# A second buffer for the converted w_a and w_b tiles of the first block

## The chip, the cores and the metric

The kernel runs on one core of one Trainium2 chip. The metric is the device time of one execution in microseconds. A number for a change is the median of several timed runs; the profile comes from one more execution, recorded by the hardware profiler, and has a time of its own.

## The reference

Three parts follow each other. Attention with a local window: 4 batches of 8 heads, 512 local and 32 global positions, head size 64; its output is a matrix x of 2304 tokens by 512. Then two feed-forward blocks:

```python
h = x @ w_in                                   # 512 -> 2048
g = where(h >= 1, h, where(h <= -1, 0, (h + 1) ** 2 / 4))
x = g @ w_out                                  # 2048 -> 512
# second block
a, b = x @ w_a, x @ w_b                        # 512 -> 1536, twice
out = (a * b) @ w_out                          # 1536 -> 512
```

The weights come in as float64, read as pairs of 32-bit words. The change concerns w_a and w_b, of 512 x 1536 each, and only their way from float64 in HBM to float32 in HBM.

## The kernel before

Tokens are cut into six tiles, five of 384 and one of 256 (a local block of 128 and the 128 global rows). The first block runs over 96 units (t, f): tile t and one of 16 slices f of the hidden size. `h_unit` makes the hidden slice with 12 matmuls of 128 x 384 into `hp` (L410 to L412) and applies the activation on ScalarE and Vector (L682 to L688); `x_unit`, two units behind, adds the slice's part of the output with 12 more matmuls into `acc`. Every matmul is threefold, since operands are split into a high and a low part.

Attention for the next tile is put between these units, one item (a block and a pair of heads) at a time: scores (L173), row minimum on Vector (L186), exponential on ScalarE (L190), normalisation (L194 to L197), transposes (L203), their copy on ScalarE (L207), the output matmuls (L213) and their copy to `xraw` (L217). From block 6 on an item also splits q and k (L160, L161).

Weights of the first block (w_in, w_out) are loaded, converted and split during tile 0, out of a pool with three raw and three converted buffers. The pool is closed when tile 1 begins, and a new one, `pc`, serves w_a and w_b: two buffers for `wraw`, the loaded tile of 128 x 512 float64, and one for `wt`, the converted tile of 128 x 512. They are turned into float32 and written to HBM (`wd`), 24 tiles in all, so that the second block can load them at half the size and several times over. The code asks for one of them in every other unit of tiles 1, 2 and 3:

```python
if i + 1 < len(ab2):
    w_load(*ab2[i + 1])                        # the load ahead, L89
(nm, f2), tf = w_conv()
nc.sync.dma_start(wd[f2]["ab".index(nm)], tf)  # L735
```

`w_conv` (L92) takes a `wt` buffer and does four instructions: L97 on ScalarE scales the high word's float, L98 shifts the bits on Vector, L99 puts the sign in, L100 the low word's bits. L97 needs the loaded tile and a free `wt` buffer. A raw buffer is free again after L100, a `wt` buffer after the write has landed. The second block reads `wd` through L500.

All these loads and writes, and those of q and k (L153) and v (L165), go through SyncE's queue. The order in which instructions stand on each engine is not that of the code: Tile puts it together when the program is built, out of the code's order, the data that each instruction needs, the buffers that are free and estimated durations. After that each engine keeps its order, and a waiting instruction holds up those behind it.

The other pools: PSUM has four buffers each for tags `h` and `acc`; `qk` has three buffers and `v` four.

Of the kernel before, what the change touches and what calls it, by code (L numbers as in the profile page):

```python
# [58 lines left out]
def body(tc, qk, vw, kg, vg, w1i, w1o, w2a, w2b, w2o, mask, out):  # L59
# [24 lines left out]
    sp = {}  # L84
    wslots = {}

    def w_load(key, src):
        raw = sp["p"].tile([P, 512, 2], I32, name="wraw", bufs=sp["raw"])
        nc.sync.dma_start(raw, src.bitcast(I32).rearrange("p (f two) -> p f two", two=2))  # L89
        wq.append((key, raw))  # L90

    def w_conv():  # L92
        key, raw = wq.pop(0)
        low, high = raw[:, :, 0], raw[:, :, 1]
        t = sp["p"].tile([P, 512], I32, name="wt", bufs=sp["wt"])
        tf = f32(t)
        nc.scalar.activation(tf, f32(high), AF.Copy, scale=W_DOWN)  # L97
        nc.vector.tensor_scalar(t, t, 3, 0x7FFFFFFF, ALU.logical_shift_left, ALU.bitwise_and)  # L98
        nc.vector.scalar_tensor_tensor(t, high, -0x80000000, t, ALU.bitwise_and, ALU.bitwise_or)  # L99
        nc.vector.scalar_tensor_tensor(t, low, 29, t, ALU.logical_shift_right, ALU.bitwise_or)  # L100
        return key, tf
# [282 lines left out]
    def x_split(t, W):  # L384
        hi, lo = [], []
        last = t == len(TILES) - 1
        for c in range(NC):
            pool = x5p if last else mp
            h = pool.tile([P, W if last else 384], F32R, name=f"xh{c}", bufs=1)
            l = pool.tile([P, W if last else 384], F32R, name=f"xl{c}", bufs=1)  # L390
            src = xraw_cur[t][c]
            nc.scalar.activation(h[:, :W], src[:, :W], AF.Copy)
            nc.vector.tensor_tensor(l[:, :W], src[:, :W], f32(h[:, :W]), ALU.subtract)  # L393
            hi.append(h)
            lo.append(l)
        return hi, lo

    def widths(t):
        return P * len(TILES[t])
# [50 lines left out]
    def x1_load(s):  # L450
        n = half_cols(s)
        t0, t1 = PAIRS[s]
        w0 = widths(t0)
        for h in range(2):
            for c in range(NC):
                r = mp.tile([P, 384], F32, name=f"x1r{h}{c}", tag=f"xh{c}" if h else f"xraw{c}", bufs=1)
                lo, hi = h * n, (h + 1) * n
                if lo < w0:
                    e = min(hi, w0)
                    nc.sync.dma_start(r[:, :e - lo], x1d[t0][c, :, lo:e])  # L460
                if hi > w0:
                    b0 = max(lo, w0)
                    nc.sync.dma_start(r[:, b0 - lo:n], x1d[t1][c, :, b0 - w0:hi - w0])
                xr[(h, c)] = r
# [28 lines left out]
    wt = {}  # L493

    def ab_load(u):

        s, f = divmod(u, NF2)
        for i in range(2):
            t = sp["p"].tile([P, 512], I32, name="wt", bufs=sp["wt"])
            nc.sync.dma_start(f32(t), wd[f][i])  # L500
            wt[(u, i)] = f32(t)
# [38 lines left out]
    def raw_to(n):  # L540
        while rawi[0] < min(n, len(ws2)):
            w_load(*ws2[rawi[0]])
            rawi[0] += 1
# [123 lines left out]
    def h_unit(t, f):  # L667
        W = widths(t)
        if t not in xs:
            xs[t] = x_split(t, W)  # L670
        hi, lo = xs[t]
        w = wslots[("i", f)]
        hp = ps.tile([P, 512], F32, name="hp", tag="h")
        for c in range(NC):
            s = slice(c * P, (c + 1) * P)
            mm3(hp[:, :W], w[:, 0, s], w[:, 1, s], hi[c][:, :W], lo[c][:, :W], c == 0, c == NC - 1)
        flush()
        r = mp.tile([P, 384], F32, name="r", tag="r", bufs=3)
        m = mp.tile([P, 384], F32, name="m", bufs=2)
        g = mp.tile([P, 2, 384], F32R, name="g", tag="g", bufs=3)  # L680
        gh, gl = g[:, 0], g[:, 1]
        nc.scalar.activation(r[:, :W], hp[:, :W], AF.Relu, bias=half, scale=0.5 / W_UP)  # L682
        nc.vector.scalar_tensor_tensor(m[:, :W], hp[:, :W], 1.0 / W_UP, r[:, :W], ALU.mult, ALU.max)  # L683
        nc.vector.scalar_tensor_tensor(m[:, :W], r[:, :W], 1.0, m[:, :W], ALU.min, ALU.mult)  # L684

        def fin():
            nc.scalar.activation(gh[:, :W], m[:, :W], AF.Copy)  # L687
            nc.vector.tensor_tensor(gl[:, :W], m[:, :W], f32(gh[:, :W]), ALU.subtract)  # L688
        deferred.append(fin)
        gq[(t, f)] = (gh, gl)  # L690
# [23 lines left out]
    for u in range(len(units)):  # L714
        for kind in (0, 1):
            if kind == 0:
                if u >= len(units):
                    continue
                t, f = units[u]
                if t == 0:  # L720
                    while W1.si < min(2 * f + LEAD1, len(ws1)):
                        W1.step()
                if t == 1 and f == 0:
                    es_st.close()
                    gp["k"] = es_att.enter_context(tc.tile_pool(name="kp", bufs=1, reuse_waits="tile"))
                    sp["p"] = es_st.enter_context(tc.tile_pool(name="pc", bufs=1, reuse_waits="tile"))
                    sp["raw"], sp["wt"] = 2, 1
                if 1 <= t <= 3 and f % 2 == 0:
                    i = 8 * (t - 1) + f // 2
                    if i == 0:  # L730
                        w_load(*ab2[0])
                    if i + 1 < len(ab2):
                        w_load(*ab2[i + 1])
                    (nm, f2), tf = w_conv()
                    nc.sync.dma_start(wd[f2]["ab".index(nm)], tf)  # L735
                if t == len(TILES) - 2 and f == 0:
                    es_st.close()
                    gp["p"] = es_att.enter_context(tc.tile_pool(name="gp", bufs=1, reuse_waits="tile"))
                if f == 0 and t + 1 < nt:
                    n_items = ends[t + 1] - done["n"]  # L740
                    rate = 3.0 * n_items / (2 * (GLOB_END if t == nt - 2 else NF1) - 1)
                    credit = 0.0
                if (t, f) == (nt - 2, GLOB_END):
                    for _ in att:
                        pass
                    es_att.close()
                    sp["p"] = es_st.enter_context(tc.tile_pool(name="st2", bufs=1, reuse_waits="tile"))
                    sp["raw"], sp["wt"] = RAWBUFS, 4
                    x5p = es_st.enter_context(tc.tile_pool(name="x5p", bufs=1, reuse_waits="tile"))
                    raw_to(RAWBUFS)  # L750
                    ab_load(0)
                if t == nt - 1 and f == 0:
                    xs[t] = xs_last
                h_unit(t, f)
                if (t, f) == (nt - 2, GLOB_END + 1):
                    xs_last = x_split(nt - 1, widths(nt - 1))
                if t == nt - 1:
                    if f == 0:
                        x1_load(0)
                    elif f == 1:  # L760
                        ab_sum(0)
                        ab_load(1)
                    elif f in (2, 3):
                        ab_split(0, 2 * f - 4)
                        ab_split(0, 2 * f - 3)
                    elif f == 4:
                        x_pre(0)
                    if f >= 5 and f < 12:
                        x_op(0, f - 5)
                    elif f == 14:  # L770
                        ab_sum(1)
                        ab_split(1, 0)
                    elif f == 15:
                        for part in range(1, 4):
                            ab_split(1, part)
            else:
                if u < LAG:
                    continue
                tx, fx = units[u - LAG]
                x_unit(tx, fx)  # L780
            if u < len(units) and t + 1 < nt:
                credit += rate
                while credit >= 1.0 and done["n"] < ends[t + 1]:
                    credit -= 1.0
                    att_step(ends[t + 1])
        if u < len(units) and f == NF1 - 1 and t + 1 < nt:
            while att_step(ends[t + 1]):
                pass
# [95 lines left out]
```

## Time and profile before

| | us |
|---|---|
| median of 3 runs | 979.52 |
| lowest and highest | 978.26, 979.92 |
| profiled execution, time | 985.52 |
| profiled execution, span | 983.7 |

| engine | busy us | share of the span |
|---|---|---|
| TensorE, matmuls (PE) | 943.9 | 96% |
| TensorE, weight loads (PEld) | 842.4 | 86% |
| Vector (DVE) | 709.4 | 72% |
| ScalarE (ACT) | 527.4 | 54% |

Busy time is the time in which at least one instruction of the engine runs; matmuls overlap in the pipeline. The span goes from the first to the last instruction, and the execution's own time has 1.8 us more. In the rows, PE is TensorE's matmuls, PEld its weight loads, DVE Vector, ACT ScalarE, SP SyncE; a q behind the name is the engine's queue. L12 is line 12 of the kernel, and "a <- b" behind an operation is what it writes and reads.

### The profile page before, as it was taken

How to read it: one execution, taken by the hardware profiler on the slowest of the kernel's cores; microseconds unless marked ns; L12 is line 12 of the kernel's file. 1: busy time of each engine (PE TensorE's matmuls, PEld its weight loads, DVE VectorE, ACT ScalarE, POOL GpSimd, SP SyncE). 2: the span in 40 equal slices, each digit the busy share in tenths (PEclk: the TensorE clock that was granted, in tenths of full speed). 3: DMA queues.
4: the chain of work that ended last, by engine and by line, in shares of the span. 5: the costliest groups of instructions: out<-in, count | busy, mean ns of one | idle time of the engine just before them, and what ended most of it. 6: DMA issues, size and time to landing. Idle time of an engine off the chain costs nothing.

```text
span 983.7 us, 16767 instructions
## 1 busy us (share of the span) xinstructions
PE 943.9 (96%) x6044; PEld 842.4 (86%) x6044; DVE 709.4 (72%) x1841; ACT 527.4 (54%) x1253; POOL 0.7 (0%) x7
## 2 busy tenths in 40 slices
PE   7899888998999999999999999999999999999997
PEld 4587677886988898898879999999999999999996
DVE  6699998877875565565446878888796666887673
ACT  7667676555555555454444655555554444644441
POOL 0000000000000000000000000000000000000000
PEclk9699999999999999999999999999999999999999
DMA  7456546554551111103435323331241111042101
GB/s 232 133 168 200 170 164 198 189 181 161 189 169 37 44 62 49 29 16 105 146 112 200 113 71 118 109 95 43 58 147 54 43 44 54 22 140 54 55 12 54
DMA packets 55843, 104.28 MB, mean 106 GB/s; under 512 B 6864, under 2 KB 28496, under 8 KB 55760
## 3 DMA queue, kind: packets, MB, share of 16 engines
q1 hardware_dynamic: 55616, 103.05, 33.6%
q8 instruction: 47, 0.77, 0.3%
q14 instruction: 36, 0.29, 0.1%
q10 hardware_dynamic: 144, 0.17, 0.1%
HBM read 87.99 MB, written 15.20 MB: 105 GB/s over the span
## 4 chain that ended last, share of the span: by engine, by line
PE 75%; DVE 10%; DMA 9%; ACT 4%; issue 2%; ACTq 0%; SPq 0%; DVEq 0%
PE hp L410 5%; PE pb L567 5%; PE pb L568 5%; PE py L632 5%; PE pb L565 5%; PE py L633 5%; PE hp L412 5%; PE acc L410 5%; PE py L631 5%; PE hp L411 5%; DMA wd<-wt 5%; PE acc L411 4%; PE acc L412 4%; PE px L565 4%; PE px L568 4%; PE px L567 4%
## 5 line engine op out<-in xcount | busy, mean ns | idle before, releaser
L410 PE MATMUL hp<-xh,w 128*128 128x384 f32 (+1 forms) x384 | 133.8, 348 | 9.7 <-DVE m L683 3.8
L410 PE MATMUL acc<-g,w 128*128 128x384 f32 (+1 forms) x384 | 133.7, 348 | 3.0 <-ACT g L687 3.0
L411 PE MATMUL acc<-g,w 128*128 128x384 f32 (+1 forms) x384 | 127.7, 333 | 0.0
L412 PE MATMUL hp<-xl,w 128*128 128x384 f32 (+1 forms) x384 | 127.2, 331 | 0.0
L411 PE MATMUL hp<-xh,w 128*128 128x384 f32 (+1 forms) x384 | 126.4, 329 | 0.0
L412 PE MATMUL acc<-g,w 128*128 128x384 f32 (+1 forms) x384 | 125.5, 331 | 0.0
L107 ACT ACTIVATE w<-wt 128x512 fp32r<-128x512 f32 (+1 forms) x116 | 65.0, 564 | 72.2 <-PE pb L568 44.8
L567 PE MATMUL pb<-w 128*128 128x384 f32 (+1 forms) x288 | 94.6, 329 | 0.0
L568 PE MATMUL pb<-w 128*128 128x384 f32 (+1 forms) x288 | 94.3, 327 | 0.0
L565 PE MATMUL pb<-w 128*128 128x384 f32 (+1 forms) x288 | 93.8, 326 | 0.0
L410 PEld LDWEIGHTS hp<-xh,w 128*128 128x128 f32 x384 | 73.0, 190 | 19.9 <-DVE m L683 5.8
L683 DVE SCALAR_TENSOR_TENSOR m<-hp,r 128x384 f32<-128x384 f32 (+1 forms) x96 | 50.9, 530 | 51.4 <-ACT r L682 51.4
L682 ACT ACTIVATE r<-hp,half 128x384 f32<-128x384 f32 (+1 forms) x96 | 53.4, 557 | 62.6 <-PE hp L412 61.9
L410 PEld LDWEIGHTS acc<-g,w 128*128 128x128 f32 x384 | 73.1, 190 | 11.7 <-issue 5.4
L687 ACT ACTIVATE g<-m 128x384 fp32r<-128x384 f32 (+1 forms) x96 | 48.3, 503 | 63.3 <-DVE m L684 63.0
L632 PE MATMUL py<-w,g 128*128 128x512 f32 x204 | 80.7, 396 | 0.0
L633 PE MATMUL py<-w,g 128*128 128x512 f32 x204 | 80.7, 396 | 0.0
L631 PE MATMUL py<-w,g 128*128 128x512 f32 x204 | 79.6, 390 | 0.0
L108 DVE TENSOR_TENSOR w<-wsum,w 128x256 fp32r<-128x256 f32 (+1 forms) x108 | 54.6, 507 | 29.3 <-ACT w L107 29.3
L411 PEld LDWEIGHTS acc<-g,w 128*128 128x128 f32 x384 | 73.1, 190 | 1.6 <-issue 1.0
L412 PEld LDWEIGHTS acc<-g,w 128*128 128x128 f32 x384 | 72.8, 190 | 1.3 <-issue 1.1
L412 PEld LDWEIGHTS hp<-xl,w 128*128 128x128 f32 x384 | 73.1, 190 | 0.8 <-DVE xl L393 0.5
(112 smaller groups left out, 2093.2 us busy)
## 6 DMA issues: line engine op xcount, KB each, us to landing
wt<-wd SPq DMA_DIRECT2D x72, 256.0 KB, 2.6
qk<-in_qk_dram SPq DMA_DIRECT2D x64, 176.0 KB, 2.5
wraw<-in_w1i_dram SPq DMA_DIRECT2D x16, 512.0 KB, 3.6
wraw<-in_w1o_dram SPq DMA_DIRECT2D x16, 512.0 KB, 4.0
v<-in_vw_dram SPq DMA_DIRECT2D x64, 112.0 KB, 2.6
wraw<-in_w2a_dram SPq DMA_DIRECT2D x12, 512.0 KB, 4.6
wraw<-in_w2b_dram SPq DMA_DIRECT2D x12, 512.0 KB, 3.8
wd<-wt SPq DMA_DIRECT2D x24, 256.0 KB, 2.2
```

Of the source, the lines that this page charges most:

```text
L107: nc.scalar.activation(hi, src, AF.Copy)
L108: nc.vector.tensor_tensor(lo, src, f32(hi), ALU.subtract)
L410: nc.tensor.matmul(acc, whi, xhi, start=first, stop=False)
L411: nc.tensor.matmul(acc, wlo, xhi, start=False, stop=False)
L412: nc.tensor.matmul(acc, whi, xlo, start=False, stop=last)
L565: nc.tensor.matmul(out[:, :n], w[:, 0, r], hi[:, c, :n], start=start and c == 0, stop=False, skip_group_check=True)
L567: nc.tensor.matmul(out[:, :n], w[:, 1, r], hi[:, c, :n], start=False, stop=False, skip_group_check=True)
L568: nc.tensor.matmul(out[:, :n], w[:, 0, r], lo[:, c, :n], start=False, stop=k in (1, 5, 6) and c == 1, skip_group_check=True)
L631: nc.tensor.matmul(a, gh[:, c], w[:, 0], start=f == 0, stop=False)
L632: nc.tensor.matmul(a, gh[:, c], w[:, 1], start=False, stop=False)
L633: nc.tensor.matmul(a, gl[:, c], w[:, 0], start=False, stop=f == NF2 - 1)
L682: nc.scalar.activation(r[:, :W], hp[:, :W], AF.Relu, bias=half, scale=0.5 / W_UP)
```

## The change

The `wt` tag of the pool `pc` gets a second buffer, from tile 1 to the end of the 24 conversions. The pool grows by 2 KB per partition. The code of a conversion and the number of raw buffers stay.

```diff
@@ -724,7 +724,7 @@
                     es_st.close()
                     gp["k"] = es_att.enter_context(tc.tile_pool(name="kp", bufs=1, reuse_waits="tile"))
                     sp["p"] = es_st.enter_context(tc.tile_pool(name="pc", bufs=1, reuse_waits="tile"))
-                    sp["raw"], sp["wt"] = 2, 1
+                    sp["raw"], sp["wt"] = 2, 2
                 if 1 <= t <= 3 and f % 2 == 0:
                     i = 8 * (t - 1) + f // 2
                     if i == 0:
```

## Rows read from the trace of the kernel before

**Rows 1.** Busy us per engine (x instructions) by stage; clock, DMA share, GB/s

```profile
core 0: us, PE busy (x) PEld busy (x) DVE busy (x) ACT busy (x) POOL busy (x), PEclk, DMA share, GB/s
100.00:140.00 40.00, 33.28 (x200) 27.88 (x200) 37.60 (x94) 26.18 (x56) 0.00 (x0) 1.00 0.57 170
160.00:170.00 10.00, 8.03 (x56) 6.92 (x56) 8.18 (x25) 6.48 (x16) 0.00 (x0) 1.00 0.73 244
150.49:287.47 136.98, 124.37 (x799) 109.90 (x798) 108.66 (x309) 81.06 (x203) 0.00 (x0) 0.98 0.57 181
287.47:446.18 158.71, 158.71 (x1058) 142.23 (x1058) 92.92 (x285) 84.18 (x214) 0.00 (x0) 1.00 0.17 49
```

**Rows 2.** The same view, ten microseconds of it

```profile
200.00:210.00 10.00, 9.49 (x55) 8.73 (x56) 8.22 (x22) 5.50 (x13) 0.00 (x0) 0.83 0.49 176
```

**Rows 3.** Shares of the chain of waits from 150 to 290 us

```profile
by line: DMA wd<-wt 31.8%; DVE wt L99 10.5%; DVE wt L100 9.0%; ACT wt L97 8.4%; issue 7.0%; DVE wt L98 5.4%; DVE m L683 4.4%; ACT e L190 3.0%; DVE g L688 2.5%; DVE e L186 2.3%; DVE qkl L161 2.0%; DVE m L684 1.8%; ACT r L682 1.6%; DVE sm L19
```

**Rows 4.** SyncE in order of time: start us, us

```profile
175.64 0.33 SPq L735 DMA_DIRECT2D wd<-wt  x1
176.08 0.36 SPq L89 DMA_DIRECT2D wraw<-in_w2a_dram  x1
...
181.46 0.34 SPq L735 DMA_DIRECT2D wd<-wt  x1
```

**Rows 5.** ScalarE in order of time, with the idle before and what ended it

```profile
177.85 0.67 ACT L97 ACTIVATE wt<-wraw 128x512 f32<-128x512 f32 x1 [0.85 <-DMA wd<-wt]
```

**Rows 6.** Who waited for whom, 140 to 290 us: total us, times, longest

```profile
ACT wt L97 <- DMA wd<-wt: 19.8, 15, 3.7
...
PE tp L203 <- DVE xraw L217: 4.1, 3, 1.7
...
PE s L173 <- ACT pt L207: 2.0, 2, 1.4
PE o L213 <- DVE mn L186: 2.0, 2, 1.1
...
PE o L213 <- DVE m L683: 1.7, 2, 0.9
...
ACT qkh L160 <- DMA qk<-in_qk_dram: 0.2, 1, 0.2
```

**Rows 7.** Instructions on wd: duration ns, first and last start us

```profile
L500 SPq DMA_DIRECT2D wt<-wd x72: 319/320/654, 519.9 to 935.4; - x72
L735 SPq DMA_DIRECT2D wd<-wt x24: 319/327/458, 150.5 to 287.0; - x24
```

**Rows 8.** A group on TensorE, 150.49 to 287.47 us: busy us, mean ns

```profile
L410 PE MATMUL acc<-g,w 128*128 128x384 f32 x80 | 29.4, 368 | 0.0
```

**Rows 9.** Vector in order of time

```profile
173.40 0.42 DVE L98 TENSOR_SCALAR wt<-wt 128x512 int32<-128x512 int32 x1
173.85 0.69 DVE L99 SCALAR_TENSOR_TENSOR wt<-wraw,wt 128x512 int32<-128x512 int32 x1
174.46 0.55 DVE L688 TENSOR_TENSOR g<-m,g 128x384 fp32r<-128x384 f32 x1
174.93 0.69 DVE L100 SCALAR_TENSOR_TENSOR wt<-wraw,wt 128x512 int32<-128x512 int32 x1
175.53 0.38 DVE L186 CUSTOM_DVE_ANT_0 e<-s,masks 128x224 f32<-128x224 f32 x1
```

**Rows 10.** DMA issues from 150.49 to 287.47 us: KB each, median us to landing

```profile
wraw<-in_w2a_dram SPq DMA_DIRECT2D x11, 512.0 KB, 4.6
wraw<-in_w2b_dram SPq DMA_DIRECT2D x11, 512.0 KB, 3.7
```

**Rows 11.** What SyncE's DMA issues waited for, whole execution

```profile
SPq L735 <- DVE wt L100: 33.2, 8, 6.7
```

**Rows 12.** Who waited for whom, whole execution

```profile
ACT wt L97 <- DMA wraw<-in_w1o_dram: 6.8, 6, 3.1
...
ACT wt L97 <- DMA wraw<-in_w1i_dram: 3.0, 3, 2.0
```

## Prediction

> **What bounds the kernel now.** I read the busy times by stage first. From 287.47 to 446.18 us TensorE has no idle time and Vector is busy 92.92 of 158.71 us, 58.5% [rows 1]. In the 136.98 us ahead of it, from the first to behind the last write of a converted tile to HBM, TensorE is busy 124.37 us and Vector 108.66, 79% [rows 1]. So this stretch holds 136.98 - 124.37 = 12.6 us of TensorE idle. The ten-microsecond stretches show two lapses of its clock, a granted 0.83 from 200 to 210 us, in the row shown, and the same from 270 to 280: about a third of each at 1.2 GHz and the rest at 2.4, 10 x 0.17 = 1.7 us of work lost each time, 3.4 together, some of which may fall into the idle [rows 2]. The reader should see a ceiling: the loss that this stretch can give back is at most 12.6 + 3.4 = 16.0 us.
>
> Then the chain of waits from 150 to 290 us. The write of a converted tile (L735) is 31.8% of it, and the four conversion instructions L97 to L100 are 8.4 + 5.4 + 10.5 + 9.0 = 33.3% [rows 3]. Two thirds of the chain is one loop: convert, write, wait for the landing, convert the next. The loop can be followed in single rows: SyncE issues the write at 175.64, ScalarE's next L97 starts at 177.85 after 0.85 us of idle that the write ended, and the next write goes out at 181.46 [rows 4, 5]. Over the stretch ScalarE waited for such a landing 15 times, 19.8 us [rows 6]. There are 24 writes between 150.5 and 287.0 us, 136.5 / 23 = 5.93 us apart, and nothing reads them before 519.9 [rows 7].
>
> The code asks for one conversion every other unit over the 48 units of tiles 1 to 3. The stretch with all 24 holds 80 of the first matmuls of an accumulation into acc, four to a unit, so 20 units [rows 8]. Tile's ordering therefore draws conversions forward to where their data and buffers allow it, and the engines' fixed order then has every one of these waits in front of softmax and activation work.
>
> **The change part by part.** It adds one tile of 512 float32 per partition and removes, for conversion i, the wait for write i-1; write i-2 is waited for instead. No instruction is added: 24 conversions and 24 writes of 256 KB stay. The second buffer's first use comes after the conversions of the first tile are over, so it costs nothing; were it to wait there, one wait of the kind of rows 6 is the bound, 19.8 / 15 = 1.3 us, which I leave out.
>
> What the wait costs cannot be more than the 16.0 us above, nor less than nothing. ScalarE's 19.8 us are no price: TensorE works through part of them.
>
> Where does the stall go? Two things are late next. One is Vector. From start to start a conversion holds it 0.45 us (L98, 173.40 to 173.85), 0.61 (L99, to 174.46) and 0.60 (L100, 174.93 to 175.53), 1.66 together [rows 9]. Where TensorE is full, the other work leaves 41.5% of Vector, so a conversion fits every 1.66 / 0.415 = 4.0 us. The other is the loop through the two raw buffers. SyncE issues the next raw load right behind the write, 0.44 us after it [rows 4]; it lands after 4.6 or 3.7 us, median of the two kinds, 4.15 as their mean [rows 10]; ScalarE takes 0.67 [rows 5], Vector 1.66 with nothing between and, by the example above, 181.46 - 177.85 = 3.6 from ScalarE's start to the write. Two conversions then take 0.44 + 4.15 + 0.67 + 1.66 = 6.9 to 0.44 + 4.15 + 3.6 = 8.2 us, 3.5 to 4.1 each. Both give 4.0 us. I take 24 x 4.0 = 96 us for the conversions in place of 137.
>
> How much does TensorE lose in these 96 us? Bounds: nothing (the stretch without conversions loses nothing), and 20% (the worst ten microseconds, 160 to 170, where TensorE was busy 8.03) [rows 1]. Between them I take today's rate, 16.0 / 136.98 = 11.7%, because Vector will be fuller (about 98% instead of 79%) while the loop through the write is gone, and I cannot see either outweigh the other. Loss after: 96 x 0.117 = 11.2 us. Gain: 16.0 - 11.2 = 4.8 us. Behind the stretch TensorE is full, so the gain passes to the end. The profiled execution took 985.52 us (983.7 of span and 1.8 around it), so 980.7 by its clock; it ran 6.0 us over the median of the three timed runs, 979.52, and I take the gain from that: **974.7 us**.
>
> TensorE's busy time overlaps between matmuls, so the size of the loss can also be read from its weight loads: 109.90 / 136.98 = 80.2% in the stretch against 142.23 / 158.71 = 89.6% behind it [rows 1]. The Trainium skill (Perfetto Trace Analysis, Identifying the Most-Contended Engine) says that matmul busy time misjudges the distance from the roofline and that the weight loads' share is to be used. By it the loss is 136.98 - 109.90 / 0.896 = 14.4 us, the gain 14.4 x 0.30 = 4.3, and the time 975.2; this trace can't tell the two sums apart.
>
> On SyncE the writes and raw loads move ahead of loads of qk and v. A write waits at the head of that queue for its L100, 33.2 us in eight such waits [rows 11], with those loads behind it. ScalarE waited only 0.2 us for a qk [rows 6], so they are covered by the three and four buffers of these tiles; if that cover went, each late qk would cost some of one landing.
>
> **The rivals.**
> *All of it comes back.* The chain of waits speaks for it: two thirds are the loop that is cut. The raw loads may wait little: in tile 0, with three raw buffers, ScalarE waited 6.8 + 3.0 = 9.8 us for 32 raw loads, 0.31 each [rows 12]; 24 such are 7.4 us against 19.8. Were TensorE's loss to shrink alike, 16.0 x 7.4 / 19.8 = 6.0 stays and 10.0 comes back, 969.5; with nothing left, 963.5. Against it: two raw buffers, not three, and a fuller Vector.
>
> *Nothing comes back.* TensorE's own idle is not put down to the write: 4.1 us to the copy of an attention output (L217), 2.0 to ScalarE's L207, 2.0 to L186 and 1.7 to L683, 9.8 of 12.6 [rows 6]. These are delays of attention steps on two busy engines, and they could stay for the same total, or the raw loop could take the write loop's place. Time 979.5. The Trainium skill (Perfetto Trace Analysis, Identifying Performance Opportunities) says that improving a kernel generally means improving its most-contended engine; TensorE is that here and the edit doesn't touch it, which would be this case.
>
> *Vector becomes the bound, and it is slower.* Conversions drawn forward at one per 4.0 us fill Vector to 98%, and each may hold up an attention or activation step by up to 0.6 us, on which TensorE's PSUM banks wait. From 100 to 140 us, where Vector is busy 37.60 of 40, TensorE is busy 33.28, 83% [rows 1]; some of that is for weights needed at once. At the 20% of the worst stretch: 96 x 0.20 = 19.2, and 3.4 x 96 / 137 = 2.4 for the clock, 21.6 in all, 5.6 more than now: 985.1. It decides from a loss of (16.0 + 2.0) / 96 = 19% on; from 17% on the gain is gone.
>
> **How the numbers follow.** A change of 0.2% (2.0 us) is about what a measurement of this kernel can tell. Forecast (gain of 2 to 9 us): 0.45, with its own range 970.5 to 977.5. All comes back (9 to 16): 0.17. Nothing (within 2): 0.16. Slower: 0.22. So faster 0.62, same 0.16, slower 0.22. For 8 in 10 the range goes from 965, most of the first rival, to 984, over half of the slower one.
>
> **What would show each step.** In the trace after: ScalarE's L97 waiting for the write near nothing instead of 19.8 us, and some 5 to 12 us for raw loads; the 24 writes over about 96 us, the last near 245 us; Vector above 90% there and near 60% from there on; TensorE idle some 9 us in it and none behind it; the write gone from the chain. The prediction is wrong upward if TensorE's idle in the stretch is over 15 us, above all behind Vector; it is wrong downward if the order spreads the conversions and TensorE idles under 5 us. It is wrong in kind if the write stays in the chain, or if the new order moves time in the parts behind 290 us, where I assume nothing.

## The result, and the profile after

| | us |
|---|---|
| before, median of 5 runs | 979.44 |
| after, median of 5 runs | 984.90 (982.89 to 986.57) |
| after / before | 1.0052, 95% interval 1.0035 to 1.0069 |
| profiled execution after, time and span | 984.9, 983.1 |

The change makes the kernel slower by 0.5%. The two profiled executions take nearly the same, 985.52 and 984.9, but the one before reached its first write of a converted tile 5.2 us later (150.49 against 145.32 us), ahead of anything that the change touches. From that write to the end of the span it is 833.2 us before and 837.8 after.

Busy times by stage answer to [rows 1]: the stretch from the first to behind the last write, and what follows it up to the end of tile 3. Columns: TensorE, its weight loads, Vector, ScalarE, GpSimd, then granted clock, DMA share, GB/s.

```profile
145.32:247.97 102.65, 85.23 (x536) 74.31 (x535) 84.41 (x235) 58.45 (x146) 0.00 (x0) 0.95 0.68 220
247.97:446.18 198.21, 198.21 (x1316) 178.04 (x1316) 117.40 (x357) 106.44 (x268) 0.00 (x0) 1.00 0.17 50
```

The 24 conversions take 102.65 us in place of 136.98. In them TensorE idles 102.65 - 85.23 = 17.4 us, against 12.6, and the granted clock is 0.95: 0.05 x 102.65 = 5.1 us lost, against 3.4 by the two lapses in the prediction (by the mean clock of that stretch, 0.02 x 136.98 = 2.7). So the loss is up to 22.5 us in place of 16.0. Behind the stretch TensorE is full, as before. Vector is busy 84.41 of 102.65, 82%: it is not full. The two ten-microsecond stretches in which TensorE is busy least, and the one with the lowest clock, which answer to [rows 2]:

```profile
160.00:170.00 10.00, 6.71 (x40) 5.72 (x39) 6.59 (x20) 4.78 (x12) 0.00 (x0) 0.85 0.72 225
...
200.00:210.00 10.00, 6.61 (x43) 5.61 (x43) 7.60 (x23) 5.22 (x14) 0.00 (x0) 1.00 0.65 202
210.00:220.00 10.00, 8.73 (x49) 7.79 (x50) 7.64 (x21) 5.75 (x15) 0.00 (x0) 0.83 0.68 227
```

The write is still issued 24 times, and nothing waits for it any more; the last one goes out at 247.5 us, 4.44 us apart, in place of 287.0 and 5.93 [rows 7]:

```profile
L735 SPq DMA_DIRECT2D wd<-wt x24: 326/327/551, 145.3 to 247.5; - x24
```

What took its place is to be seen in the chain of waits from 140 to 255 us, which answers to [rows 3]:

```profile
by line: DMA wraw<-in_w2a_dram 40.2%; DVE wt L100 8.2%; DVE wt L99 7.4%; ACT wt L97 5.9%; issue 5.1%; DVE e L186 4.4%; DVE wt L98 3.8%; DVE qkl L161 2.6%; PE hp L410 2.2%; DVE m L683 2.1%; PE hp L411 1.7%; PE hp L412 1.7%; DVE xl L393 1.6%;
```

The write is gone from it and the load of a w_a tile, absent before, is 40.2%. Who waited for whom, 140 to 260 us, answers to [rows 6]:

```profile
ACT wt L97 <- DMA wraw<-in_w2a_dram: 20.0, 10, 3.3
DVE wt L98 <- ACT wt L97: 14.0, 16, 2.5
...
PE o L213 <- DVE mn L186: 5.5, 4, 3.3
...
PE s L173 <- DVE m L683: 3.7, 4, 1.5
...
ACT wt L97 <- DMA wraw<-in_w2b_dram: 0.8, 2, 0.5
```

ScalarE waited 20.8 us for raw loads, where it had waited 19.8 for writes. The wait moved one buffer back, at full size. It doesn't stay on ScalarE: L98 of the conversion stands in Vector's own order, and Vector waited there for the late L97 in 16 places, 14.0 us of its 102.65 - 84.41 = 18.2 us of idle. The kernel before has the same line, 140 to 290 us:

```profile
DVE wt L98 <- ACT wt L97: 16.1, 16, 2.1
```

One such wait can be followed to TensorE, in rows of ScalarE, Vector and TensorE:

```profile
205.68 0.67 ACT L97 ACTIVATE wt<-wraw 128x512 f32<-128x512 f32 x1 [3.27 <-DMA wraw<-in_w2a_dram]
...
206.37 0.43 DVE L98 TENSOR_SCALAR wt<-wt 128x512 int32<-128x512 int32 x1 [1.97 <-ACT wt L97]
...
207.44 0.38 DVE L186 CUSTOM_DVE_ANT_0 e<-s,masks 128x224 f32<-128x224 f32 x1
...
207.89 0.66 PE L213 MATMUL o<-pt,v 112*64 112x128 f32 x8 [1.18 <-DVE mn L186]
```

L97 is late by a load, Vector stands before L98, an attention item's L186 behind it is late, and TensorE waits for that. How a late L97 comes about shows in single rows, SyncE first, then ScalarE (compare [rows 4, 5]):

```profile
209.21 0.33 SPq L735 DMA_DIRECT2D wd<-wt  x1
209.63 0.38 SPq L89 DMA_DIRECT2D wraw<-in_w2a_dram  x1
...
213.52 0.33 SPq L735 DMA_DIRECT2D wd<-wt  x1
```

```profile
210.43 0.66 ACT L97 ACTIVATE wt<-wraw 128x512 f32<-128x512 f32 x1
210.99 0.52 ACT L687 ACTIVATE g<-m 128x384 fp32r<-128x384 f32 x1
214.56 0.67 ACT L97 ACTIVATE wt<-wraw 128x512 f32<-128x512 f32 x1 [3.06 <-DMA wraw<-in_w2a_dram]
```

At 209.63 SyncE issues a w_a load, right behind the write of the conversion that freed its raw buffer. The w_b tile in the other buffer is converted at 210.43. The instruction after the next is already L97 for the load just issued, and it stands at the head of the queue from 211.5 to 214.56, 3.06 us, with the softmax of an attention item behind it. The order put this L97 where a load would have to land in about 2 us (209.63 to 211.5); it took 4.9. Why the order did so is not shown; that it reckoned with shorter loads is a guess from this place. The loads themselves are as long as before [rows 10]:

```profile
wraw<-in_w2a_dram SPq DMA_DIRECT2D x11, 512.0 KB, 4.6
wraw<-in_w2b_dram SPq DMA_DIRECT2D x11, 512.0 KB, 3.6
```

### The profile page after: what moved, and what is told of

The parts are those of the page before. It is cut to its first block, busy times and chain, and to the rows that moved or that the text cites. A ratio compares the mean times of both kernels' runs of the same rounds, so it can differ in the third digit from the quotient of the medians.

```text
span 983.1 us, 16759 instructions
## 1 busy us (share of the span) xinstructions
PE 941.9 (96%) x6044; PEld 842.3 (86%) x6044; DVE 710.5 (72%) x1841; ACT 527.3 (54%) x1253; POOL 0.7 (0%) x7
## 4 chain that ended last, share of the span: by engine, by line
PE 80%; DVE 8%; DMA 7%; ACT 3%; issue 1%; SPq 0%; ACTq 0%; DVEq 0%
PE hp L410 6%; PE acc L410 5%; PE hp L412 5%; PE hp L411 5%; PE acc L411 5%; PE pb L567 5%; PE pb L568 5%; PE pb L565 5%; PE py L632 5%; PE py L633 5%; PE acc L412 5%; DMA wraw<-in_w2a_dram 5%; PE py L631 5%; PE px L565 4%; PE px L568 4%; PE px L567 4%
## 5 line engine op out<-in xcount | busy, mean ns | idle before, releaser
L410 PEld LDWEIGHTS hp<-xh,w 128*128 128x128 f32 x384 | 73.5, 191 | 18.2 <-DVE m L683 4.4
L410 PEld LDWEIGHTS acc<-g,w 128*128 128x128 f32 x384 | 72.7, 189 | 11.9 <-issue 5.8
L411 PEld LDWEIGHTS acc<-g,w 128*128 128x128 f32 x384 | 72.8, 190 | 1.6 <-issue 1.0
L411 PEld LDWEIGHTS hp<-xh,w 128*128 128x128 f32 x384 | 73.9, 192 | 0.0
```

The source lines that it names most:

```text
L410: nc.tensor.matmul(acc, whi, xhi, start=first, stop=False)
L411: nc.tensor.matmul(acc, wlo, xhi, start=False, stop=False)
```

## The experiments

Two theories stood against each other: that the loss comes from L97 waiting at the head of ScalarE's queue for something not yet landed (A), and that it comes from conversions crowding Vector and ScalarE (B). Times are medians; ratios are to runs of the kernel before on the same chip. Conversions are held back by a hold on the order: L97 of conversion i may be queued on ScalarE only behind the activation of a given unit.

```diff
-        nc.scalar.activation(r[:, :W], hp[:, :W], AF.Relu, ...)
+        relus.append(nc.scalar.activation(r[:, :W], hp[:, :W], AF.Relu, ...).ins)
...
-                    (nm, f2), tf = w_conv()
+                    with tc.issue_after(relus[NF1 + i - 1]):       # one per unit
+                        (nm, f2), tf = w_conv()
```

In the table, "apart" is the distance of the writes, first to last over 23; "L97 waits" is what ScalarE waited there for loads and writes; "idle" is TensorE's idle from 140 to 430 us of the profiled execution, a window that holds the writes of every kernel. In three kernels (raw3_wt1, half_raw4_wt3, half_raw4_unit08) the view puts some waits of L97 down to Vector or to "issue"; in each of these the write that frees the buffer landed 0.1 us or less before L97 began, so they are counted as waits for the write. In the kernels with half loads, L97 is L104 and L98 is L105 in the rows.

| kernel | raw, wt | apart us | L97 waits us | idle us | time us | ratio to before, 95% |
|---|---|---|---|---|---|---|
| before | 2, 1 | 5.93 | 19.8 | 12.6 | 979.44 | |
| after | 2, 2 | 4.44 | 20.8 | 17.4 | 984.90 | 1.0052 (1.0035 to 1.0069) |
| raw3_wt1 | 3, 1 | 5.93 | 19.9 | 13.2 | 978.44 | 0.9981 (0.9965 to 0.9997) |
| unit1_wt1, one per unit | 2, 1 | 6.20 | 15.9 | 8.7 | 976.58 | 0.9958 (0.9940 to 0.9975) |
| unit1_wt2, one per unit | 2, 2 | 5.74 | 0.5 | 1.9 | 964.67 | 0.9854 (0.9827 to 0.9882) |
| unit2_wt1, one per two units | 2, 1 | 11.3 | 0 | 1.6 | 964.97 | 0.9839 (0.9817 to 0.9861) |
| unit2_wt2, one per two units | 2, 2 | 11.3 | 0 | 1.5 | 964.52 | 0.9844 (0.9808 to 0.9881) |
| unit08_wt2, five per four units | 2, 2 | 5.23 | 11.1 | 11.0 | 979.46 | 0.9994 (0.9976 to 1.0011) |
| half_raw2_wt2, half loads | 2, 2 | 4.08 | 16.8 | 14.4 | 982.41 | 1.0021 (1.0001 to 1.0040) |
| half_raw4_wt2, half loads | 4, 2 | 3.38 | 8.2 | 8.8 | 972.82 | 0.9931 (0.9909 to 0.9953) |
| half_raw4_wt3, half loads | 4, 3 | 3.11 | 12.0 | 9.5 | 977.46 | 0.9966 (0.9947 to 0.9985) |
| raw3_y2 | 3, 2 | in bursts | 15.9 | 10.2 | 974.51 | 0.9936 (0.9915 to 0.9958) |
| half_raw4_unit08, five per four units | 4, 2 | 4.83 | 4.3 | 5.6 | 972.83 | 0.9923 (0.9893 to 0.9953) |
| half_raw4_unit1, one per unit | 4, 2 | 5.77 | 0 | 2.4 | 965.16 | 0.9857 (0.9830 to 0.9884) |
| half_raw4_unit08_no_l99 | 4, 2 | 4.57 | 0.3 | 1.5 | 964.67 | 0.9834 (0.9811 to 0.9858) |
| after_no_l99 | 2, 2 | 3.78 | 14.9 | 12.5 | 980.61 | 1.0002 (0.9983 to 1.0020) |

### The raw buffer alone

```diff
-                    sp["raw"], sp["wt"] = 2, 2
+                    sp["raw"], sp["wt"] = 3, 1
```

> Three raw buffers and one converted buffer: the raw buffer alone, without the change. Theory A (waits in the fixed order: the loss comes from L97 standing at the head of ScalarE's queue before the thing it waits for has landed): the write loop still binds as in the kernel before, L97 waits 15 to 25 us for the write, time 977 to 982. Theory B (crowding: the loss comes from how many conversions per microsecond Vector and ScalarE get, waits or not): conversions stay one per 5.9 us, time 979.5 as before.

Writes still 5.93 us apart, and a gain of 0.2% whose interval ends just short of nothing. The waits, 140 to 290 us:

```profile
ACT wt L97 <- DMA wd<-wt: 14.7, 13, 3.7
...
ACT wt L97 <- issue: 3.7, 1, 3.7
...
ACT wt L97 <- DVE x L709: 1.5, 1, 1.5
```

With the two that the view names otherwise, 14.7 + 3.7 + 1.5 = 19.9 us of waits for writes, as many as before, and as A expected. The write loop did bind the kernel before, as read from its chain.

### One conversion per unit, with one buffer and with two

The hold above, with `2, 1` and `2, 2`.

> One converted buffer, and conversion i is queued on ScalarE behind the activation of unit 16 + i - 1, so at most one per unit, about the pace that the kernel before has in the trace (one per 5.9 us). Theory A: the write loop (5.7 us) is just as long as a unit with its attention item (5.65), so some 10 to 20 us of waits for the write stay, time 976 to 981. Theory B: same pace, same loss, 979.5.

> The change (two converted buffers), with the same hold: conversion i behind the activation of unit 16 + i - 1. A pair of conversions then takes 11.3 us, against 8.9 for the loop through the raw buffers in the changed kernel, so L97 meets neither a write nor a load that is late. Theory A: waits of L97 under 3 us, TensorE idle in the stretch under 5 us, time 966 to 971. Theory B: the pace of the kernel before, so its loss too, 977 to 982.

With one buffer, the waits for the write stay, from the trace from 140 to 291 us:

```profile
ACT wt L97 <- DMA wd<-wt: 15.9, 9, 3.6
```

With two, hardly any is left, and TensorE idles 132.50 - 130.58 = 1.9 us in the stretch. Waits, then the stretch by busy times:

```profile
ACT wt L97 <- DMA wraw<-in_w2a_dram: 0.5, 1, 0.5
```

```profile
145.10:277.60 132.50, 130.58 (x864) 115.73 (x865) 113.16 (x328) 86.45 (x216) 0.00 (x0) 1.00 0.59 190
```

Vector is busy 113.16 of 132.50 us here, 85%, more than the 82% of the changed kernel, and TensorE hardly stops. So theory B in its plain form falls: the same pace as before, no loss. A's numbers were met, but for a time 1 us under its range with two buffers. Nor is the larger pool the reason for the loss: this kernel has the buffers of the changed one. The second buffer, harmful as it was put in, is here worth 0.9958 - 0.9854 = 1.0%, 10 us, for 15.4 us of waits: 0.66 us for each (by the two intervals, 0.45 to 0.87).

### One conversion every other unit

The hold with `relus[NF1 + 2 * i - 1]`.

> One converted buffer, and conversion i is queued behind the activation of unit 16 + 2 i - 1: one every other unit, the place where the code asks for it. A write has 11.3 us to land. Theory A: no waits of L97, TensorE idle under 5 us, time 966 to 971, the same as one per unit with two buffers. Theory B: half the pace of the kernel before, so about half of its loss, 971 to 974, and clearly below one per unit with two buffers.

> Two converted buffers, one conversion every other unit. Theory A: with the write no longer waited for, the second buffer has nothing to remove, so the time of one buffer at this pace, 965.0, within 1.5. Theory B gives the same here; the run shows whether the second buffer costs or gains anything by itself.

All three kernels with next to no waits and at most one conversion per unit take the same, within their intervals: 1.5% less than before. That is the ceiling of 16.0 us that the prediction read from the stretch (0.9839: 15.8 us). With a conversion every other unit one buffer does as well as two; its 964.97 us lie 1 us under A's range and clear of B's.

### Five conversions in four units

The hold with `relus[NF1 + 4 * i // 5 - 1]`, full loads.

> Two converted buffers, conversion i held behind the activation of unit 16 + floor(0.8 i) - 1: five conversions in four units, about one per 4.5 us, the density that the changed kernel has (4.44 us) without its waits being given by the ordering. Theory A (waits in the fixed order): a pair has 9.0 us against some 8 for the loop through the raw buffers, so few waits, 2 to 8 us in all, time 965 to 971. Theory B (crowding): the density of the changed kernel, so its time, 982 to 987.

A's numbers were missed. Two of every five conversions share a unit under this hold, and loads are late again, 140 to 420 us:

```profile
ACT wt L97 <- DMA wraw<-in_w2b_dram: 7.0, 6, 1.8
...
ACT wt L97 <- DMA wraw<-in_w2a_dram: 4.1, 4, 2.0
```

### Half loads

To open the loop through the raw buffers without more room, each load brings half of the columns, and the conversion reads them twice; four such buffers take the room of two.

```diff
-        raw = sp["p"].tile([P, 512, 2], I32, name="wraw", bufs=sp["raw"])
+        n = 256 if key[0] in "ab" else 512
+        raw = sp["p"].tile([P, n, 2], I32, name="wraw", bufs=sp["raw"])
+        src = src[:, :n]
```

> The changed kernel with two raw buffers, each load of w_a and w_b only the first 256 of 512 columns (256 KB in place of 512), which the conversion reads twice, so the second half of these weights is left out and replaced by the first. Theory A: a load lands after about 2.6 us in place of 4.2, closer to what the order allows for; waits for raw loads fall from 20.8 to 5 to 12 us, time 970 to 978, although conversions come faster. Theory B: conversions one per 3.6 to 4.0 us, more crowded than in the changed kernel, 985 to 992.

> The same half loads (the second half of w_a and w_b left out, replaced by the first), and four raw buffers of half the size, so the room is that of the changed kernel. The loop through the raw buffers is cut: no load is waited for. Theory A: L97 waits only for the write, at most 5 us in all, and TensorE idles under 6 us although conversions come as densely as Vector lets them, time 964 to 971. Theory B: the densest order of all, 985 to 995.

With two buffers the waits for loads fall by only 4 us and the conversions move closer; the half loads landed after 2.8 (w_a) and 3.5 us (w_b), not 2.6. The time lies between the two theories' numbers. With four, conversions come one per 3.38 us and now wait for the write, 8.2 us. The stretch, then the waits of ScalarE and of Vector:

```profile
142.50:220.70 78.20, 69.45 (x449) 59.96 (x448) 76.19 (x213) 53.09 (x129) 0.00 (x0) 0.98 0.63 201
```

```profile
ACT wt L104 <- DMA wd<-wt: 8.2, 10, 1.2
...
DVE wt L105 <- ACT wt L104: 0.2, 1, 0.2
```

Vector is busy 76.19 of 78.20 us, 97%, and the kernel is still faster than before. TensorE idles 8.8 us, which neither theory alone had foretold. Here Vector hardly waits for a late conversion, 0.2 us against 14.0 in the changed kernel.

> Half loads (the second half of w_a and w_b left out, replaced by the first), four raw and three converted buffers: L97 meets neither a late load nor a late write, and conversions come as densely as the order lets them, one per 3.3 us or less. Theory A: no waits, no loss, 964 to 967. Theory B: the 8.8 us of TensorE idle that two converted buffers left are from the density and stay, 972 to 976.

The third buffer let the order put conversions 3.11 us apart, and they waited for the write again, 10.1 + 1.2 + 0.7 = 12.0 us: slower than with two. The premise, that nothing is waited for, did not hold, so this run separates nothing; it repeats the pattern of the change.

### Full loads, three raw buffers and two converted ones

```diff
+        if key[0] in "ab":
+            t = mp.tile([P, 512], F32, name="wt", tag="y", bufs=2).bitcast(I32)
...
-                    sp["raw"], sp["wt"] = 2, 2
+                    sp["raw"], sp["wt"] = 3, 0
```

> Full loads, three raw buffers and two converted ones (the two take the room of another tag's two buffers, which serves elsewhere only at the end of a tile): the change, with the loop through the raw buffers opened too. Theory A (waits in the fixed order alone): L97's waits for loads fall from 20.8 to under 6 us, TensorE idle under 6 us, time 966 to 972, though conversions come at one per 3.5 to 4 us. Theory B (crowding alone): denser than the changed kernel, 985 to 990. Both in part, as half loads with four buffers (972.8) suggest: 972 to 978.

The borrowed room is needed at the end of each tile, and so the conversions came in three bursts, the writes of the last two about 3 us apart. No load was waited for, but writes and stores of tile outputs were, 15.9 us. The time is in the range for both causes in part.

### Pace without waits

> Half loads (the second half of w_a and w_b left out, replaced by the first) with four raw and two converted buffers, and conversion i held behind the activation of unit 16 + floor(0.8 i) - 1: the pace of the held kernel with full loads that took 979.5, without its 11.1 us of waits. Theory A: waits under 1 us, idle under 3 us, 964 to 967. Theory B: pace decides, so 977 to 981.

> Half loads (the second half of w_a and w_b left out, replaced by the first), four raw and two converted buffers, one conversion per unit. If the 972.8 of the same kernel at 0.8 units is the price of density, this one takes 964 to 966, as with full loads (964.7). If half loads or four buffers cost something by themselves, 970 to 974.

> Half loads (the second half of w_a and w_b left out), four raw and two converted buffers, conversion i held behind unit 16 + floor(0.8 i) - 1, and L99 left out in these conversions (no sign bits), 0.6 us less of Vector each. If the density costs through Vector, the time falls from 972.8 to 965 to 969. If it costs through ScalarE or the order alone, it stays at 971 to 974.

> The changed kernel without L99 in the conversions of w_a and w_b (their sign bits are left out), so 1.05 us of Vector in place of 1.66 each. The load loop stays, a pair some 1.2 us shorter. Theory A: a load is late by as much as before, waits of 15 to 25 us, TensorE idle 14 to 20, time 982 to 988. Theory B: 24 x 0.6 = 15 us less work for Vector, idle down by a third or more, time 974 to 979.

At one conversion per unit, half loads take 0.9857, the same as full loads, as expected. At five per four units they take 0.9923, between A's numbers and B's: 0.66% more, 6.5 us (2.5 to 10.4 by the two intervals). Without L99 the same hold gives 0.9834, 964.67 us, just under the range for a price through Vector. But A's premise, waits under 1 us, did not hold in the second of these kernels. Its waits, 140 to 260 us:

```profile
ACT wt L104 <- DVE m L698: 1.9, 1, 1.9
...
ACT wt L104 <- DMA wd<-wt: 1.6, 3, 0.7
...
ACT wt L104 <- DVE wt L105: 0.8, 1, 0.8
```

The first of them ends at 244.91 us; the write that frees its buffer goes out at 241.82 and lands after 3.0 us. So it, too, is a wait for a write, and all of them are 1.9 + 1.6 + 0.8 = 4.3 us, against none at one per unit and 0.3 without L99. At 0.66 each they are 2.8 of the 6.5 us, and the 3.7 that are left lie within the interval. So a price of the pace by itself is not shown, nor that it is Vector's: leaving out L99 took the waits along with Vector's work. The stretch from 140 to 260 us with L99, then without:

```profile
140.00:260.00 120.00, 114.58 (x740) 101.29 (x738) 106.03 (x297) 77.09 (x193) 0.00 (x0) 0.99 0.51 160
```

```profile
140.00:260.00 120.00, 118.50 (x783) 105.79 (x780) 97.52 (x284) 81.90 (x200) 0.00 (x0) 0.99 0.53 174
```

TensorE idles 5.4 us in the first, with Vector busy 106.03 of 120 us, and 1.5 in the second, with 97.52. The full-load kernel under the same hold took 0.9994, so its 11.1 - 4.3 = 6.8 us more of waits cost 7.0 us, 1.0 for each (0.5 to 1.5 by the two intervals). The last run, the changed kernel without L99, tells nothing apart: its waits fell by 5.9 us along with Vector's work, and its time lies between the two theories' numbers.

## Why the prediction was wrong

The text forecast 4.8 us of gain, 974.7 us, and gave a slower outcome 0.22; measured were 984.90 us and a loss.

- **What bounds the kernel.** Right. The loop through the write bound the stretch, and its loss had a ceiling of 16.0 us: kernels without the waits and without crowding came down by 14.3 to 15.8 us.
- **The write is no longer waited for.** Right: none after, 19.8 us before. The conversions take 102.65 us; 96 was the estimate.
- **What the 96 us lose.** This is the step that failed: "I take today's rate, 16.0 / 136.98 = 11.7%, because Vector will be fuller (about 98% instead of 79%) while the loop through the write is gone, and I cannot see either outweigh the other." 11.2 us of loss were estimated; 22.5 are in the trace. The loop through the raw buffers had been worked out, at 3.5 to 4.1 us per conversion, and used only for the length of the stretch. It was not asked where the order would put L97 against that loop. It put it up to 3 us too early, as it had put it too early against the write. Waits for loads were expected at 5 to 12 us, were given no price in the sum, and came to 20.8. The sign named beforehand for an error upward, over 15 us of TensorE idle, came: 17.4.
- **Vector.** Expected above 90%, measured 82%: Vector itself waited 14.0 us for late L97s. The "about 98%" of the text doesn't follow from its terms, either: 24 x 1.66 = 39.8 of 96 us are 41%, and 58.5% for the rest at 88.3% of TensorE's pace are 52%, 93% together. The slower rival gave 985.1, and that this is near the 984.9 measured is luck: it came to it by a full Vector. The kernel with Vector at 97% was faster than the one before, so a full Vector is not by itself the reason. Its part of the mechanism, that conversions drawn closer hold up attention steps on Vector without any wait for a DMA, stays open.
- **The sum that the runs support.** By the ratios the changed kernel lies 1.0052 - 0.9854 = 2.0%, 19.4 us, over the held one, and the kernel before 14.3. That the early order is what costs them is shown: with the same buffers and the hold, the waits and the loss are gone. How they divide is not. At 0.66 us for each, the 20.8 us of waits are 13.7 of the 19.4, and the 19.8 of the kernel before 13.1 of its 14.3; at 1.0 they would be more than all of both. So one price for the waits doesn't give the 5.1 us between the two kernels. The closer pace is one candidate, what stands behind each late L97 another; each edit that took the waits moved the pace as well, so none tells them apart.
- **The rivals that cost nothing.** *All of it comes back* was reached only with a hold. *Nothing comes back* had the mechanism half right: the raw loop did take the write loop's place, with waits as long, but at a higher cost.
- **Behind the stretch.** As assumed, nothing moved: TensorE is full up to the end of tile 3 in both.

## What to carry to other kernels

A buffer added to work that an ordering pass draws forward need not only remove a wait: here it let the pass draw the work closer, up to the next buffer, and the next wait was as long as the last (20.8 us after 19.8). A third buffer beside half loads did the same. Before adding the buffer, ask whether the work is due at all; here nothing read the result for over 200 us, and holding it to its place in the code, with one buffer, gave 1.6%, where the second buffer alone cost 0.5%.

## What the runs showed of the hardware

A late DMA is paid for on engines that don't wait for it themselves. In the changed kernel ScalarE waits 20.8 us for loads, Vector 14.0 us for the instruction that ScalarE held back, and TensorE 5.5 us for the row minimum (L186) that Vector holds, each in its own fixed order.

The granted clock was 0.95 in the changed kernel's stretch, where TensorE idles 17.4 of 102.65 us, with single lapses to 0.83 and 0.85, and 1.00 in the held kernel, whose TensorE had 1.9 us of idle in 132.5. One lapse in detail: TensorE idles 3.4 us of the ten from 200 to 210 us, at a granted 1.00, and the next ten have 0.83; matmuls of 384 columns, which start 0.17 us apart at 206 us, start 0.32 us apart from 212 to 214. In the changed kernel that clock accounts for up to 5.1 of the 22.5 us, a part that the sum of idle times doesn't show.
